# A hand-pipelined transformer block becomes a list of single-engine steps

## The chip, the cores and the metric

The kernel runs on one core of a Trainium2 chip. The metric is the device time of one execution in microseconds; the profiled execution also gives the span and every instruction's start and duration. The engines are PE (TensorE; PEld are its weight loads), DVE (VectorE), ACT (ScalarE), POOL (GpSimd) and SP (SyncE, which here only issues transfers). Each works through its own list of instructions.

## The reference

One block with a modulation from a condition vector: linear attention with softmax features, then a gated MLP that mixes along the sequence. S = 2048 rows, D = 448, 16 heads of 28, all in bf16.

```python
sa, ca, ga, sb, cb, gb = split(silu(c) @ w_mod, 6)
h = layernorm(x) * (1 + ca) + sa
q, k, v = split(h @ wqkv)
pq, pk = q @ w_phi, k @ w_phi                       # per head, 28 x 28
phi_q, phi_k = [softmax(pq), softmax(-pq)], [softmax(pk), softmax(-pk)]
kv, z = phi_k.T @ v, phi_k.sum(rows)
x = x + ga * ((phi_q @ kv) / (phi_q @ z + 1e-6)) @ wo
h = layernorm(x) * (1 + cb) + sb
zz = gelu(h @ w_in); z1, z2 = zz[:, :896], layernorm(zz[:, 896:])
x = x + gb * ((z1 * (w_sp @ z2 + b_sp)) @ w_out)
```

## The kernel before

`fast_path` does the work; `general_path` (not printed) runs only if a flag, read near the end, says that a bound is exceeded. Rows are 16 tiles of 128. Weights are folded on the chip: w_phi goes into wk and wq (`fold_T`, `fold_pf`), and the modulation goes into the weights. The scale 1+ca multiplies the rows of Wk, Wq and Wv, the shift sa becomes an extra row 64 of their last block through `fold_sa` and `bias_row`, and the transposed activations carry a one in column 448 (xpad, lines 578 to 580). For w_in, `win_bias` and `win_scale` do the same. `apply_ln` (L637) writes the normalised tile to xpad, and a DMA transpose on SP turns it into hT or h2T.

The order is written by hand. Setup runs to line 738. The k loop (L893) gives each tile k, v, their exps, sums (L762), reciprocal, phik (L766) and, two tiles later, the kv accumulation; loads, statistics of later tiles and weight folds are placed by tile number (`loads`, `late`). Half of q is done inside, the rest after it. `slot(j)` (L1042) is a software pipeline over tiles: num and its normalisation (L939 to 972), wo with the residual (L974), second layernorm, z2 (L1015) with bn_stats on DVE (L989) and the normalisation on ACT (L1012), z1 (L1030). Last come 28 g units of 16 matmuls (L1109) and the output products (L1118). The 32 w_sp transposes are issued on SP: five late in the k loop, eleven in the slots, sixteen before the g stage. Four one-bank and two two-bank PSUM buffers are handed out in rotation. The guard bounds the column norms of the folded weights (`norm_sq`, `norm_mm`).

Of the kernel before, what the change touches and what calls it, by code (L numbers as in the profile page):

```python
# [475 lines left out]
KB = [P, P, P, D - 3 * P + 1]  # L476
HP = 4
CB = HP * DH
BOUND = 1.9


def fast_path(tc, A_x, A_wqkv, A_w_phi, A_wo, B_w_in, B_w_sp, B_b_sp, B_w_out, c, w_mod, out, flag):

# [3 lines left out]
    NST = S // 512  # L489
# [17 lines left out]
    win_s = persist.tile([P, KC, 2 * FH], BF, name="f_win")
# [52 lines left out]


    nc.sync.dma_start(out=c_row[:], in_=c)
    nc.scalar.dma_start(out=x_sb[:, 0:2, :], in_=xv[:, 0:2, :])
    load_rows(nc.sync, wk_raw[:, :, 0:D], A_wqkv[:, D:2 * D])
    nc.scalar.dma_start(out=wm1[:, :, D:960], in_=wmod_v[:, :, D:960])
    with nc.allow_non_contiguous_dma(reason="small w_phi blocks"):
        nc.sync.dma_start(out=phi[:], in_=A_w_phi.rearrange("(g l) d f -> (l d) g f", l=4))
    nc.sync.dma_start(out=wm1[:, :, 0:D], in_=wmod_v[:, :, 0:D])
    load_rows(nc.sync, wv_raw, A_wqkv[:, 2 * D:3 * D])


    nc.vector.memset(warm[:], 0.0)
    nc.vector.memset(sbpad[:], 0.0)
    nc.scalar.activation(out=warm[:], in_=warm[:], func=ACT.Exp)
    make_identity(nc, ident[:])
    nc.gpsimd.memset(wk_raw[:, :, D:D + 16], 0.0)
    nc.gpsimd.memset(mhalf[:], -0.5)
    for r in range(4):
        nc.gpsimd.memset(xpad[r][:, D:512], 0.0)
        nc.gpsimd.memset(xpad[r][:, D:D + 1], 1.0)  # L580
    nc.gpsimd.memset(sapad[:], 0.0)
    with nc.allow_low_precision("0/1 masks are exact in bf16"):
        nc.vector.tensor_reduce(out=bmask[:], in_=ident[0:CB, 0:CB].rearrange("p (h f) -> p h f", h=HP), axis=AX.X, op=ALU.add)
        nc.vector.tensor_reduce(out=mask[:], in_=ident[:].rearrange("p (k h) -> p h k", h=HP), axis=AX.X, op=ALU.add)
    for s in range(2):
        nc.vector.tensor_copy(out=KVbd[:, s, :, :, 29], in_=mask[:].unsqueeze(1).to_broadcast([P, 4, HP]))

    def more_constants():
        for r in range(4, NX):
            nc.gpsimd.memset(xpad[r][:, D:512], 0.0)  # L590
            nc.gpsimd.memset(xpad[r][:, D:D + 1], 1.0)
        nc.gpsimd.memset(wq_raw[:, :, D:D + 16], 0.0)
        nc.gpsimd.memset(Wq[:, :, D:D + 16], 0.0)
        for r in range(3):
            nc.gpsimd.memset(pring[r][:, 2 * D:2 * D + 16], 0.0)
            nc.gpsimd.memset(vring[r][:, :, DH:DH + 1], 1.0)
        nc.gpsimd.memset(ones[:], 1.0)
        for r in range(NO):
            nc.gpsimd.memset(opad[r][:, D:512], 0.0)


# [12 lines left out]
    def keep_busy(n):
        wps = bank2("warm_ps")
        for _ in range(n):
            nc.tensor.matmul(wps[:, 0, :], lhsT=ident[:], rhs=sbpad[:].rearrange("p k m -> p (k m)"), start=True, stop=True)

    keep_busy(7)


    def stats_of(src, mv_t, tagp, pool):
        stats = pool.tile([P, nc.vector.BN_STATS_DIM], F32, tag=tagp + "st")
        nc.vector.bn_stats(out=stats[:], in_=src)
        nc.vector.bn_aggr(out=mv_t, in_=stats[:])

    def rstd_of(mv, n, tagp):
        rstd = sm.tile([P, 2], F32, tag=tagp + "rs")
        nc.gpsimd.tensor_scalar(out=rstd[:, 0:n], in0=mv[:, 0:n, 1], scalar1=LN_EPS, scalar2=None, op0=ALU.add)
        nc.gpsimd.tensor_tensor(out=rstd[:, 0:n], in0=rstd[:, 0:n], in1=mhalf[:, 0:n], op=ALU.pow)  # L630
        nmr = sm.tile([P, 2], F32, tag=tagp + "nm")
        for t in range(n):
            nc.gpsimd.tensor_scalar(out=nmr[:, t:t + 1], in0=mv[:, t, 0:1], scalar1=rstd[:, t:t + 1], scalar2=-1.0,
                                    op0=ALU.mult, op1=ALU.mult)
        return rstd, nmr

    def apply_ln(eng, i, rstd, nmr, t, dst):  # L637
        xp = xpad[i % NX]
        eng.tensor_scalar(out=xp[:, 0:D], in0=x_sb[:, i, :], scalar1=rstd[:, t:t + 1], scalar2=nmr[:, t:t + 1],
                          op0=ALU.mult, op1=ALU.add)  # L640
        nc.sync.dma_start_transpose(out=dst, in_=xp[:])

    l1mv, l1rs = {}, {}

    def l1_stats(i):
        if i % 2 == 0:
            l1mv[i // 2] = sm.tile([P, 2, nc.vector.BN_AGGR_DIM], F32, name="l1mv", tag="l1mv")
        stats_of(x_sb[:, i, :], l1mv[i // 2][:, i % 2, :], "l1", sm)

    def l1_rstd(q):  # L650
        l1rs[q] = rstd_of(l1mv.pop(q), 2, "l1")

    def l1_apply(i, eng):
        rstd, nmr = l1rs[i // 2]
        apply_ln(eng, i, rstd, nmr, i % 2, hT[:, :, i * P:(i + 1) * P])


    def fold_T(wraw, wT, act):
        tps = [bank_bf("tps") for _ in range(4)]
        for ms in ((0, 1, 2), (3,)):  # L660
            for g in range(4):
                for m in ms:
                    nc.tensor.transpose(tps[g][:, m * P:m * P + KD[m]], wraw[0:KD[m], m, g * CB:g * CB + P],
                                        ident[0:KD[m], 0:KD[m]])
        for g in range(4):
            if act or g % 2 == 0:
                nc.scalar.copy(out=wT[:, g, 0:D], in_=tps[g][0:CB, 0:D])
            else:
                nc.vector.tensor_copy(out=wT[:, g, 0:D], in_=tps[g][0:CB, 0:D])

    def fold_sa(wraw, wT):
        sa_ps = bank("sa_ps")
        for g in range(4):
            for kk in range(KC):
# [48 lines left out]
    for m in range(3):  # L723
        fold_pf(wTk, Wk, m, m % 2)
# [314 lines left out]
    def on(i):  # L1039
        return 0 <= i < NT  # L1040
# [164 lines left out]
```

## Time and profile before

| | |
|---|---|
| runs shown | 290.99, 290.8, 289.18 us (median 290.8) |
| span of the profiled execution | 288.6 us, 4323 instructions |
| transfers | 25.81 MB, of these 17.76 MB on SP's queue, 7.69 MB on ACT's |

The page gives no time for the profiled execution beside its span; the median run is 2.2 us above it. Section 1 of the page has busy time by engine, section 4 the chain of work that ended last, section 5 groups of instructions: busy us, mean ns of one, and after the bar the idle time before them with what ended it. Matmuls are pipelined, so a row's mean for one (379 ns for 512 columns) is longer than the distance between two (3.45 us for 16 in the chain).

### The profile page before, as it was taken

The numbers are of one execution on the slowest core, as the hardware profiler recorded it, in microseconds if no ns is written. First come the engines' busy times: TensorE is split into PE (matmuls) and PEld (weight loads), VectorE is DVE, ScalarE is ACT, GpSimd is POOL, SyncE is SP. The second block draws the span as 40 slices with busy tenths as digits, with TensorE's granted clock in tenths as the row PEclk, the third lists the DMA queues.
The fourth block names the chain that finished last, engine by engine and source line by source line (L and its number), as shares of the span: only waits on it lengthen the run. The fifth ranks groups of instructions, "written<-read, shape, count | busy, mean of one in ns | idle before, by whom it ended". The sixth has DMA issues, their size and how long they took to land.

```text
span 288.6 us, 4323 instructions
## 1 busy us (share of the span) xinstructions
PE 265.1 (92%) x1514; PEld 131.1 (45%) x1538; DVE 169.0 (59%) x353; ACT 111.2 (39%) x206; POOL 93.3 (32%) x197
## 2 busy tenths in 40 slices
PE   6688979995996989999999999999999999999991
PEld 3535544553442445444444444444444444444440
DVE  4587978798478799887754343334343343434333
ACT  2446648688684568676788800000000000000000
POOL 4544676620047667766554740000000000000000
PEclk9759999999798899999999999999999999999998
DMA  8929984384012765897635999000000000000102
GB/s 208 264 39 227 279 111 131 76 146 54 2 36 55 112 130 116 122 222 143 93 58 139 169 162 198 11 2 16 32 16 2 16 32 18 0 16 16 35 2 69
DMA packets 71088, 25.81 MB, mean 89 GB/s; under 512 B 61009, under 2 KB 70930, under 8 KB 71058
## 3 DMA queue, kind: packets, MB, share of 16 engines
q1 hardware_dynamic: 64098, 17.76, 34.6%
q10 hardware_dynamic: 6960, 7.69, 9.9%
q8 instruction: 14, 0.23, 0.4%
q14 instruction: 16, 0.13, 0.2%
HBM read 8.92 MB, written 1.84 MB: 37 GB/s over the span
## 4 chain that ended last, share of the span: by engine, by line
PE 75%; DMA 9%; DVE 8%; ACT 2%; issue 2%; POOL 1%; SPq 0%; DVEq 0%; ACTq 0%; POOLq 0%
PE g_ps L1113 33%; PE o_ps L1120 7%; PE z_ps L1034 7%; PE z_ps L1021 7%; PE k_ps L748 4%; PE x_ps L979 3%; DMA f_hT<-f_xpad 3%; PE q_ps L797 3%; PE v_ps L756 2%; DMA h2T<-f_xpad 2%; PE b_ps L705 2%; DMA f_phi<-in_A_w_phi_dram 2%; PE q_ps L784 2%; DVE sums L762 2%; PE kvacc L774 2%
## 5 line engine op out<-in xcount | busy, mean ns | idle before, releaser
L1113 PE MATMUL g_ps<-f_wsp,f_z2n 128*128 128x512 bf16 x437 | 97.9, 379 | 0.6
L1113 PEld LDWEIGHTS <-f_z2n 128*128 128x128 bf16 x448 | 43.8, 98 | 52.2
L1115 DVE TENSOR_TENSOR gb<-g_ps,f_bsp 128x512 f32<-128x512 f32 x28 | 19.4, 691 | 69.7 <-PE g_ps L1113 63.7
L1021 PE MATMUL z_ps<-f_win,h2T 128*128 128x448 bf16 (+1 forms) x128 | 28.4, 366 | 3.9 <-DVE t L966 3.4
L1034 PE MATMUL z_ps<-h2T,f_win 128*128 128x512 bf16 (+1 forms) x106 | 25.8, 380 | 0.5 <-issue 0.3
L968 POOL TENSOR_TENSOR f_opad<-t 128x448 bf16<-128x448 bf16 x16 | 16.5, 1031 | 25.3 <-DVE t L966 25.2
L989 DVE BATCH_NORM_STATS2 stats<-z2g 128x6 f32<-128x448 bf16 x32 | 18.3, 615 | 10.5 <-ACT z2g L1027 10.5
L1120 PE MATMUL o_ps<-f_wout,f_z1T 128*128 128x448 bf16 x112 | 23.3, 352 | 0.0
L1027 ACT ACTIVATE z2g<-z_ps 128x896 bf16<-128x896 f32 x16 | 14.7, 917 | 16.3 <-PE z_ps L1021 16.3
L1116 DVE TENSOR_TENSOR f_z1T<-gb,f_z1T 128x512 bf16<-128x512 f32 x28 | 19.7, 704 | 1.4
L762 DVE TENSOR_REDUCE sums<-f_E 128x32 f32<-128x896 bf16 x16 | 17.1, 1070 | 5.0 <-ACT f_E L751 4.9
L1021 PEld LDWEIGHTS <-h2T 128*128 128x128 bf16 (+1 forms) x128 | 12.3, 99 | 15.4 <-issue 3.2
L1012 ACT ACTIVATE f_z2n<-z2g,nm,rs 128x896 bf16<-128x896 bf16 x16 | 18.1, 1132 | 1.6 <-POOL nm L999 1.6
L966 DVE TENSOR_TENSOR t<-num,w 128x896 bf16<-128x896 f32 x16 | 17.5, 1091 | 1.5
L748 PE MATMUL k_ps<-f_Wk,f_hT 128*128 128x448 bf16 x64 | 16.1, 381 | 1.2 <-DMA f_hT<-f_xpad 0.7
L979 PE MATMUL x_ps<-f_wo,oT 128*128 128x448 bf16 x64 | 16.4, 354 | 0.6 <-DMA oT<-f_opad 0.4
L1120 PEld LDWEIGHTS <-f_z1T 128*128 128x128 bf16 x112 | 11.0, 98 | 10.9
L1034 PEld LDWEIGHTS <-f_win 128*128 128x128 bf16 x112 | 10.1, 97 | 12.8 <-issue 2.0
L756 PE MATMUL v_ps<-f_Wv,f_hT 128*128 128x448 bf16 x64 | 14.7, 354 | 0.9 <-DVE f_wTq L677 0.9
L1035 ACT ACTIVATE f_z1T<-z_ps 128x512 bf16<-128x512 f32 x28 | 15.1, 590 | 0.5 <-PE z_ps L1034 0.5
L766 DVE TENSOR_TENSOR f_phik<-f_E,r 128x896 bf16<-128x896 bf16 x16 | 12.6, 789 | 1.2
L996 POOL TENSOR_TENSOR rs<-rs,f_mhalf 128x2 f32<-128x2 f32 (+1 forms) x19 | 12.6, 664 | 1.6
(130 smaller groups left out, 331.6 us busy)
## 6 DMA issues: line engine op xcount, KB each, us to landing
out_dram<-ot SPq DMA_DIRECT2D x16, 112.0 KB, 1.7
f_x<-in_A_x_dram ACTq DMA_DIRECT2D x3, 448.0 KB, 4.8
f_win<-in_B_w_in_dram ACTq DMA_DIRECT2D x2, 672.0 KB, 6.0
f_wm<-in_w_mod_dram ACTq DMA_DIRECT2D x1, 840.0 KB, 6.8
f_wmg<-in_w_mod_dram ACTq DMA_DIRECT2D x2, 392.0 KB, 3.6
f_wout<-in_B_w_out_dram ACTq DMA_DIRECT2D x1, 784.0 KB, 5.4
f_wsp<-in_B_w_sp_dram SPq DMA_TRANSPOSE x32, 4.0
f_bsp<-in_B_b_sp_dram ACTq DMA_DIRECT2D x1, 512.0 KB, 3.8
```

Source lines behind the costliest of these rows:

```text
L748: nc.tensor.matmul(k_ps[:, 0:D], lhsT=hT[0:KB[kc], kc, i * P:(i + 1) * P], rhs=Wk[0:KB[kc], kc, :], start=(kc == 0), stop=(kc == KC - 1))
L756: nc.tensor.matmul(v_ps[:, 0:D], lhsT=hT[0:KB[kc], kc, i * P:(i + 1) * P], rhs=Wv[0:KB[kc], kc, :], start=(kc == 0), stop=(kc == KC - 1))
L762: nc.vector.tensor_reduce(out=sums[:], in_=E[:].rearrange("p s (c f h) -> p (s c) h f", c=4, h=HP), axis=AX.X, op=ALU.add)
L979: nc.tensor.matmul(x1[:, 0:D], lhsT=oT[0:KD[cc], cc, :], rhs=wo_s[0:KD[cc], cc, :], start=False, stop=(cc == KC - 1))
L989: nc.vector.bn_stats(out=stats[:, hf, :], in_=z2gs[i][:, hf, :])
L1012: nc.scalar.activation(out=z2n[:, i, :], in_=z2gs.pop(i)[:].rearrange("p a d -> p (a d)"), func=ACT.Identity, scale=rstd[:, 1:2], bias=nmr ...
L1021: nc.tensor.matmul(z_ps[:, hf, 0:D], lhsT=h2[0:KB[kc], kc, il * P:(il + 1) * P], rhs=win_s[0:KB[kc], kc, FH + hf * D:FH + (hf + 1) * D], s ...
L1034: nc.tensor.matmul(z_ps[:], lhsT=win_s[0:KB[kc], kc, fc * P:(fc + 1) * P], rhs=h2[0:KB[kc], kc, :], start=(kc == 0), stop=(kc == KC - 1))
L1113: nc.tensor.matmul(g[:], lhsT=z2n[:, s_, fc * P:(fc + 1) * P], rhs=wsp_tiles[tcn][:, s_, :], start=(s_ == 0), stop=(s_ == NT - 1))
L1115: nc.vector.tensor_tensor(out=gb[:], in0=g[:], in1=bsp[:, tsl], op=ALU.add)
L1116: nc.vector.tensor_tensor(out=z1T[:, fc, tsl], in0=gb[:], in1=z1T[:, fc, tsl], op=ALU.mult)
L1120: nc.tensor.matmul(o_ps, lhsT=z1T[:, fc, t * P:(t + 1) * P], rhs=wout_s[:, fc, :], start=(fc == 0), stop=(fc == FC - 1))
```

## The change

The body of `fast_path` is replaced. Each step becomes a function that runs on one engine, and a string, ORDER, lists 832 steps in the order in which they are issued; `/V`, `/S`, `/G`, `/Y` choose DVE, ACT, POOL or SP, `@A0` to `@A2` and `@B0`, `@B1` name the PSUM buffer (two banks or one).

- Layernorm's scale and shift are applied to the transposed tile in place (`fmod`: f1, f2), by DVE, ACT or POOL. The row of ones, the bias matmuls and the weight scalings go.
- Tiles 0 and 1 are transposed by PE (`X`) and scaled on the way out of PSUM (`XE`).
- Seven of the eight pieces of w_sp's first quarter (`W:0,u`) are loaded in the setup, ahead of the first DMA transpose of a tile (`T1:3`); w_sp's later quarters go into the space of Eq and hT.
- phik (`kP`) runs on POOL for nine tiles and on DVE for seven. The num normalisation (`nS`) runs for pairs of tiles, on POOL for two of eight pairs.
- The residual is added by PE for seven tiles (`wN`) and by DVE for nine (`wM`, `wR/V`). Sums for the second layernorm and for z2's come from accumulator outputs (`wR`, `wQ`, `zG`, `zQ`, the squares on ACT), moments from four small DVE steps for two tiles, the power on POOL; z2's normalisation (`zN`) is on DVE.
- The guard takes the largest of all softmax sums instead of the weights' norms, in the g stage.
- The last four output products end one after another.

```diff
-KB = [P, P, P, D - 3 * P + 1]
-BOUND = 1.9
+SUM_MAX = 4.0e12
+ORDER = """
+ld:c/Y ld:x0/S ld:wk/Y ld:wma1/S ld:x1/S du:4@A2 ld:phi/Y ld:x2/S m3 ld:wma2/Y ld:x3/S ct@B0 ld:wv/Y tbl m1 l1s:0 du:12@A2 m4 W:0,4 ce:1 ce:2 ce:3
+ce:4 W:0,2 l1r:0,1 FTk:0@B0 W:0,0 bd/G FTk:1@B1 l1a:0/V ETk:0/V W:0,5 X:0@A2 m2 ETk:1/S du:4@A1 l1s:1 cfA@B0 W:0,3 l1s:2 l1r:1,2 l1s:3 W:0,6 PFk:1@B1
+ec1 PFk:0@A1 l1r:2,4 l1a:1/V EPk:1/S PFk:2@A0 ec2 l1s:4 W:0,7 XE:0,3/S X:1@B0 PFk:3@B1 XE:0,0/S l1a:3/G EPk:2/V XE:0,1/S XE:0,2/V T1:3 EPk:3/S l1s:5
+vM:0@A2 EPk:0/S l1s:6 XE:1,3/S kM:0@B1 vC:0 l1s:7 XE:1,0/S ld:wq/Y kE:0 XE:1,1/V l1r:4,8 l1a:2/V kF:0 ld:x4/Y XE:1,2/V kM:1@B0 T1:2 ld:wo/S kS:0
...
+"""
+    def fmod(a, b, m, eng, sc, sh):
+        v = hT[:, m, a * P:b * P]
+        affine(eng, v, v, sc[:, m:m + 1], sh[:, m:m + 1])
+    def nS(j, eng):
+        cr, dn, w = crr[j % 2], dnr[j % 2], wr[j % 2]
+        eng.tensor_tensor(out=dn[:], in0=cr[:, :, 0, :], in1=cr[:, :, 1, :], op=ALU.add)
+        if eng is nc.gpsimd:
+            eng.tensor_tensor(out=dn[:], in0=dn[:], in1=mone[:].unsqueeze(2).to_broadcast([P, 2, H]), op=ALU.pow)
+        else:
+            eng.reciprocal(out=dn[:], in_=dn[:])
+        eng.tensor_tensor(out=w[:], in0=Sx[:, 2 * j:2 * j + 2], in1=dn[:].unsqueeze(2).to_broadcast([P, 2, 2, H]), op=ALU.mult)
+    def kP(i, eng):
+        eng.tensor_tensor(out=pr[i % NR][:, 0:2 * D].rearrange("p (a f h) -> p a f h", a=8, h=HP),
+                          in0=Er[i % NR][:].rearrange("p s (c f h) -> p (s c) f h", c=4, h=HP),
+                          in1=kr[i % 2][:].unsqueeze(2).to_broadcast([P, 8, DH, HP]), op=ALU.mult)
+    def zG(i):
+        nc.scalar.activation(out=stage_b()["z2g"][i % NZ][:], in_=ps["z" + str(i)][:, :, 0:D], func=ACT.Gelu_apprx_tanh, accum_out=zs1[:, i:i + 1])
+    def zQ(i):
+        nc.scalar.activation(out=junk[:], in_=later["z2g"][i % NZ][:].rearrange("p a d -> p (a d)"), func=ACT.Square, accum_out=zs2[:, i:i + 1])
+    for word in ORDER.split():
...
+            STEPS[nm](*[int(v) for v in arg.split(",") if v], **kw)
```

More of the change, by code (lines that the diff above doesn't have):

```diff
@@ L569, in fast_path @@
[L569 to L589, printed above, removed]
-            nc.gpsimd.memset(xpad[r][:, D:512], 0.0)
-            nc.gpsimd.memset(xpad[r][:, D:D + 1], 1.0)
-        nc.gpsimd.memset(wq_raw[:, :, D:D + 16], 0.0)
+    def load_phi(eng):
+        with nc.allow_non_contiguous_dma(reason="small w_phi blocks"):
+            eng.dma_start(out=phi[:], in_=A_w_phi.rearrange("(g l) d f -> (l d) g f", l=4))
@@ new lines, in ld, with consts @@
+    def ld(nm, eng):
+        LOADS[nm](eng)
+    def consts():
+        nc.vector.memset(one1[:], 1.0)
+        nc.vector.memset(warm[:], 0.0)
+        nc.vector.memset(zero[:], 0.0)
+        make_identity(nc, ident[:])
+        nc.gpsimd.memset(mhalf[:], -0.5)
+        for r in range(2):
+            nc.gpsimd.memset(xpad[r][:, D:512], 0.0)
+        nc.gpsimd.memset(hT[64:P, 3, 0:2 * P], 0.0)
+        with nc.allow_low_precision("0/1 masks are exact in bf16"):
+            nc.vector.tensor_reduce(out=bmask[:], in_=ident[0:CB, 0:CB].rearrange("p (h f) -> p h f", h=HP), axis=AX.X, op=ALU.add)
+            nc.vector.tensor_reduce(out=mask[:], in_=ident[:].rearrange("p (k h) -> p h k", h=HP), axis=AX.X, op=ALU.add)
@@ L619, in fast_path @@
[L619 to L648, printed above, removed]
@@ L735, in fast_path @@
-    l1_stats(4)
-    l1_stats(5)
-    l1_rstd(2)
-    l1_apply(4, nc.gpsimd)
-    Eq = eqp.tile([P, 4, 2, S], BF, name="f_Eq")
-    kvacc = bank2("kvacc")
-    qt = {}
-    def k_part(i):
-        k_ps = bank("k_ps")
-        for kc in range(KC):
-            nc.tensor.matmul(k_ps[:, 0:D], lhsT=hT[0:KB[kc], kc, i * P:(i + 1) * P], rhs=Wk[0:KB[kc], kc, :], start=(kc == 0), stop=(kc == KC - 1))
-        E = Ering[i % 3]
-        nc.scalar.activation(out=E[:, 0, :], in_=k_ps[:, 0:D], func=ACT.Exp)
-        nc.scalar.activation(out=E[:, 1, :], in_=k_ps[:, 0:D], func=ACT.Exp, scale=-1.0)
@@ L770, in kv_acc, with scb_copy, du @@
-    def kv_acc(i):
+        nc.gpsimd.memset(mone[:], -1.0)
+        nc.gpsimd.memset(ones[:], 1.0)
+        for s in range(2):
+            nc.gpsimd.tensor_copy(out=KVbd[:, s, :, :, 29], in_=mask[:].unsqueeze(1).to_broadcast([P, 4, HP]))
+        nc.gpsimd.memset(wo_s[64:P, 3, :], 0.0)
+        nc.gpsimd.memset(win_s[64:P, 3, :], 0.0)
+    def scb_copy():
+        nc.gpsimd.tensor_copy(out=scb[:], in_=scol[:].unsqueeze(2).to_broadcast([DC, KC, P]))
+    ps = {}
+    def du(n, slot):
+        wps = bank(slot, "warm_ps")
+        for _ in range(n):
+            nc.tensor.matmul(wps[:, 0, 0:256], lhsT=zero[:, 0:P], rhs=zero[:, 0:256], start=True, stop=True)
@@ new lines, in tbl, with ct, ctv, ce @@
+    def tbl():
+        nc.scalar.activation(out=warm[:], in_=warm[:], func=ACT.Exp)
+    def ct(slot):
+        t = ps["ct"] = bank_bf(slot, "ct_ps")
+        for kk in range(KC):
+            nc.tensor.transpose(t[0:DC, 2 * kk:2 * kk + 1], c_row[0:1, kk * DC:(kk + 1) * DC], one1[:])
+    def ctv():
+        return ps["ct"][0:DC, 0:8].rearrange("p (k t) -> p k t", t=2)[:, :, 0]
+    def ce(n):
+        if n == 1:
+            nc.scalar.activation(out=e[:], in_=ctv(), func=ACT.Exp, scale=-1.0)
+        elif n == 2:
+            nc.vector.tensor_scalar(out=e[:], in0=e[:], scalar1=1.0, scalar2=None, op0=ALU.add)
+        elif n == 3:
+            nc.vector.reciprocal(out=e[:], in_=e[:])
+        else:
+            nc.vector.tensor_tensor(out=scol[:], in0=e[:], in1=ctv(), op=ALU.mult)
@@ new lines, in kM, with kE, vM @@
+    def kM(i, slot):
+        t = ps["k" + str(i)] = bank(slot, "k_ps")
+        for m in range(KC):
+            nc.tensor.matmul(t[:, 0, 0:D], lhsT=hT[:, m, i * P:(i + 1) * P], rhs=Wk[:, m, :], start=(m == 0), stop=(m == KC - 1))
+    def kE(i, s):
+        nc.scalar.activation(out=Er[i % NR][:, s, :], in_=ps["k" + str(i)][:, 0, 0:D], func=ACT.Exp, scale=1.0 - 2.0 * s)
+    def vM(i, slot):
+        t = ps["v" + str(i)] = bank(slot, "v_ps")
+        for m in range(KC):
+            nc.tensor.matmul(t[:, 0, 0:D], lhsT=hT[:, m, i * P:(i + 1) * P], rhs=wv[:, m, :], start=(m == 0), stop=(m == KC - 1))
@@ L933, in fast_path, with qE @@
-    q_one(10)
-    q_one(11)
-    nums, sxs, oTs, h2Ts, x1s, z2ps, z2gs, mvs, rss = {}, {}, {}, {}, {}, {}, {}, {}, {}
-    def num_mm(i):
-        n_ps = bank2("num")
+            for m in range(KC):
+                nc.tensor.matmul(t[:, u, :], lhsT=Wq[:, m, cc * CB:cc * CB + P], rhs=hT[:, m, st * 512:(st + 1) * 512],
+                                 start=(m == 0), stop=(m == KC - 1))
+    def qE(n, s):
+        st, c2 = divmod(n, 2)
+        nc.scalar.activation(out=Eq[st // 2][0:CB, 2 * c2:2 * c2 + 2, s, (st % 2) * 512:(st % 2 + 1) * 512], in_=ps["q" + str(n)][0:CB, :, :],
+                             func=ACT.Exp, scale=1.0 - 2.0 * s)
@@ L1003, in l2_apply @@
-    def l2_apply(i, j):
-        st, il = divmod(i, 4)
-        if il == 0:
-            h2Ts[st] = sm2.tile([P, KC, 512], BF, name="h2T", tag="h2T", bufs=2)
-        rstd, nmr = rss[j]
-        apply_ln(nc.gpsimd, i, rstd, nmr, 0, h2Ts[st][:, :, il * P:(il + 1) * P])
-    def z2_norm(i, j):
-        rstd, nmr = rss[j]
-        nc.scalar.activation(out=z2n[:, i, :], in_=z2gs.pop(i)[:].rearrange("p a d -> p (a d)"), func=ACT.Identity,
-                             scale=rstd[:, 1:2], bias=nmr[:, 1:2])
@@ new lines, in wM, with wR @@
+    def wM(i, slot, with_x):
+        t = ps["x" + str(i)] = bank(slot, "x1_ps")
+        if with_x:
+            nc.tensor.matmul(t[:, 0, 0:D], lhsT=ident[:], rhs=x_sb[:, i, :], start=True, stop=False)
+        for cc in range(KC):
+            nc.tensor.matmul(t[:, 0, 0:D], lhsT=oTr[i % 4][:, cc, :], rhs=wo_s[:, cc, :], start=(cc == 0 and not with_x), stop=(cc == KC - 1))
+    def wR(i, eng):
+        t = ps["x" + str(i)][:, 0, 0:D]
+        if eng is nc.scalar:
+            nc.scalar.activation(out=x_sb[:, i, :], in_=t, func=ACT.Copy, accum_out=s1[:, i:i + 1])
+        else:
+            nc.vector.scalar_tensor_tensor(out=x_sb[:, i, :], in0=t, scalar=1.0, in1=x_sb[:, i, :], op0=ALU.mult, op1=ALU.add,
+                                           accum_out=s1[:, i:i + 1])
@@ new lines, in rpow, with l2a, T3, zM @@
+    def rpow(a, b, v):
+        nc.gpsimd.tensor_tensor(out=v[:, a:b], in0=v[:, a:b], in1=mhalf[:, 0:b - a], op=ALU.pow)
+    def l2a(i, eng):
+        eng.tensor_scalar(out=xpad[(NT + i) % NX][:, 0:D], in0=x_sb[:, i, :], scalar1=m2[:, i:i + 1], scalar2=v2[:, i:i + 1],
+                          op0=ALU.add, op1=ALU.mult)
+    def T3(i):
+        nc.sync.dma_start_transpose(out=hT[:, :, i * P:(i + 1) * P], in_=xpad[(NT + i) % NX][:])
+    def zM(i, slot):
+        t = ps["z" + str(i)] = bank(slot, "z2_ps")
+        for hf in range(2):
+            for m in range(KC):
+                nc.tensor.matmul(t[:, hf, 0:D], lhsT=hT[:, m, i * P:(i + 1) * P], rhs=win_s[:, m, FH + hf * D:FH + (hf + 1) * D],
+                                 start=(m == 0), stop=(m == KC - 1))
@@ new lines, in zN, with yM @@
+    def zN(i, eng):
+        z2n = stage_b()["z2n"]
+        eng.tensor_scalar(out=z2n[:, i, :], in0=later["z2g"][i % NZ][:].rearrange("p a d -> p (a d)"), scalar1=zm[:, i:i + 1], scalar2=zv[:, i:i + 1],
+                          op0=ALU.add, op1=ALU.mult)
+    def yM(st, fc, slot):
+        t = ps["y%d_%d" % (st, fc)] = bank(slot, "z1_ps")
+        for m in range(KC):
+            nc.tensor.matmul(t[:, 0, :], lhsT=win_s[:, m, fc * P:(fc + 1) * P], rhs=hT[:, m, st * 512:(st + 1) * 512], start=(m == 0), stop=(m == KC - 1))
@@ new lines, in yG, with W, gM @@
+    def yG(st, fc):
+        nc.scalar.activation(out=stage_b()["z1T"][:, fc, st * 512:(st + 1) * 512], in_=ps["y%d_%d" % (st, fc)][:, 0, :], func=ACT.Gelu_apprx_tanh)
+    def W(t, u):
+        q, hf = divmod(u, 2)
+        r0 = t * TCHF + q * P
+        nc.sync.dma_start_transpose(out=wspT[t][:, hf * 8:(hf + 1) * 8, q * P:(q + 1) * P], in_=B_w_sp[r0:r0 + P, hf * 1024:(hf + 1) * 1024])
+    def gM(t, fc, slot):
+        g = ps["G%d_%d" % (t, fc)] = bank(slot, "g_ps")
+        for s_ in range(NT):
+            nc.tensor.matmul(g[:, 0, :], lhsT=later["z2n"][:, s_, fc * P:(fc + 1) * P], rhs=wspT[t][:, s_, :], start=(s_ == 0), stop=(s_ == NT - 1))
@@ new lines, in gG, with oM @@
+    def gG(t, fc):
+        gb = later["gb"][fc % 2]
+        z = later["z1T"][:, fc, t * TCHF:(t + 1) * TCHF]
+        nc.vector.tensor_tensor(out=gb[:], in0=ps["G%d_%d" % (t, fc)][:, 0, :], in1=bsp[:, t * TCHF:(t + 1) * TCHF], op=ALU.add)
+        nc.vector.tensor_tensor(out=z, in0=gb[:], in1=z, op=ALU.mult)
+    def oM(t, f0, f1, slot):
+        if f0 == 0:
+            ps["o" + str(t)] = bank(slot, "o_ps")
+        for fc in range(f0, f1):
+            nc.tensor.matmul(ps["o" + str(t)][:, 0, 0:D], lhsT=later["z1T"][:, fc, t * P:(t + 1) * P], rhs=wout_s[:, fc, :], start=(fc == 0), stop=(fc == FC - 1))
@@ L1157, in fast_path @@
+    later["zp"].release()
+    psp.release()
+    eqp.release()
     persist.release()
-    return over
-TCHF = 512
+    return later["over"]
 def kernel(
```

758 lines of the change are left out of this document (300 added, 458 removed).

## The prediction

> **What bounds the kernel now.** I read the page first, then busy time by stage, the chain in order of time, the groups by form, the DMA rows and one stretch of the timeline. The page names the bound on average:
>
> ```profile
> PE 265.1 (92%) x1514; PEld 131.1 (45%) x1538; DVE 169.0 (59%) x353; ACT 111.2 (39%) x206; POOL 93.3 (32%) x197
> ```
>
> That average hides five stages. Their ends come from the timeline: first k matmul 15.6, first num matmul (KVbd is written) 77.6, first z2 matmul 92.4, first g matmul 164.7, last matmul 282.7 us.
>
> ```profile
> 0.00:15.60 15.60, 10.38 (x93) 6.69 (x94) 8.36 (x30) 5.28 (x10) 7.40 (x43) 0.83 0.96 219
> 15.60:77.60 62.00, 55.37 (x403) 30.34 (x409) 49.56 (x90) 41.23 (x74) 26.74 (x45) 0.93 0.60 124
> 77.60:92.40 14.80, 12.43 (x91) 6.10 (x90) 11.18 (x31) 10.96 (x30) 7.23 (x12) 1.00 0.17 39
> 92.40:164.70 72.30, 69.62 (x380) 33.36 (x387) 52.20 (x133) 52.09 (x92) 47.25 (x94) 0.98 0.70 129
> 164.70:282.70 118.00, 117.26 (x549) 54.57 (x558) 46.16 (x70) 1.61 (x2) 4.65 (x5) 1.00 0.20 36
> ```
>
> Columns: stretch, length, busy us (instructions) of PE, PEld, DVE, ACT, POOL, then granted clock, DMA share, GB/s. Only the fourth stretch (z) and the fifth (g) are PE's: in the g stage PE is busy for 117.3 of 118.0 us, while in the k stage it leaves 6.6 us idle, runs at a clock of 0.93, and DVE is at 80%. In the chain, setup and the k stage hang on transfers and on DVE:
>
> ```profile
> 7.42 8.15 DMA f_hT<-f_xpad
> ...
> 15.62 3.17 PE k_ps L748 x8
> ...
> 26.74 0.98 DVE sums L762
> ...
> 42.85 0.76 PE k_ps L748 x4
> ...
> 123.56 5.60 DMA h2T<-f_xpad
> ...
> 277.24 5.31 PE o_ps L1120 x28
> ```
>
> The first transpose waits 8.15 us behind earlier loads (median of that kind: 3.7); the first k matmuls take 3.17 us for 8, later ones 0.76 for 4, so the clock is at half there.
>
> ```profile
> L1012 ACT ACTIVATE f_z2n<-z2g,nm,rs 128x896 bf16<-128x896 bf16 x16 | 18.1, 1132 | 1.6 <-POOL nm L999 1.6
> L762 DVE TENSOR_REDUCE sums<-f_E 128x32 f32<-128x896 bf16 x16 | 17.1, 1070 | 5.0 <-ACT f_E L751 4.9
> L968 POOL TENSOR_TENSOR f_opad<-t 128x448 bf16<-128x448 bf16 x16 | 16.5, 1031 | 25.3 <-DVE t L966 25.2
> L996 POOL TENSOR_TENSOR rs<-rs,f_mhalf 128x2 f32<-128x2 f32 x13 | 9.2, 708 | 1.1
> L996 POOL TENSOR_TENSOR rs<-rs,f_mhalf 128x1 f32<-128x1 f32 x6 | 3.4, 568 | 0.5
> ```
>
> **The change, part by part.** I sum against this execution's span, 288.6 us; the runs shown have median 290.8, 2.2 above it, and I carry those 2.2 over.
>
> *PE work.* Gone: 20 bias matmuls (4 take 0.76: 3.8 us), 8 norm matmuls (1.5), 32 one-column ones (16 take 1.12: 2.2), 9 of 16 identity matmuls (0.19 each: 1.7). New: 8 small transposes (0.4). Warm-ups hold as many columns as before. That is 8.8 us less, but most lies in the k stage, which PE does not bound, so I credit it only through the stages below.
>
> *Setup and k stage.* Tiles 0 and 1 no longer wait for a DMA transpose; PE transposes them, so the first k comes some 3 us earlier. Behind them SP's queue now holds seven w_sp transposes ahead of T1:3 and T1:2, which tile 2 needs; the loads of wq and of x tiles 8 to 11 stand between those two. PE's order has the fold of wq, kv of tile 0 and k of tile 2 next, all behind these transfers, so PE will stand from about 20 to 28 us. Transfers before T1:14, the last one: 7.26 MB of loads at 269 GB/s (stretch 5 to 10 us) 27.0 us; 7 w_sp pieces at 1.51 us (ten were issued in 15.13 us from 155.5 on) 10.6; 14 tile transposes of 131 KB at 159 GB/s (that stretch's rate) 0.82 each, 11.5. Together 49.1; with the first issue and 2 to 3 us of landing, T1:14 is there at 52. Then three shift-and-scale steps on POOL (512 columns, from 0.71 for 448: 0.81 each), k and its exp (1.5), on DVE four times sums and reciprocal (1.07+0.35) and three phik (0.62), 7.5 us, the last kv matmuls and KVbd (2.2): 66.5. Bounds: DVE's own 16 tiles from 12 us on give 57; transfers at the landing time of a single piece instead (4.0 each) give 84. I take 66.5, nearer the issue spacing, since these pieces follow each other as those ten did.
>
> *POOL beside DVE.* Nine of 16 phik go to POOL, at twice L968's 1031 ns. One stretch shows a cost:
>
> ```profile
> 46.28 0.93 POOL L883 TENSOR_TENSOR f_wk_raw<-f_Wk 65x448 bf16<-65x448 bf16 x1
> ...
> 46.39 2.89 DVE L766 TENSOR_TENSOR f_phik<-f_E,r 128x896 bf16<-128x896 bf16 x1
> ...
> 47.20 0.70 POOL L639 TENSOR_SCALAR f_xpad<-f_x,rstd,nmr 128x448 bf16<-128x448 bf16 x1
> ...
> 47.87 0.93 POOL L883 TENSOR_TENSOR f_wq_raw<-f_Wq 128x448 bf16<-128x448 bf16 x1
> ```
>
> A DVE step of 0.62 took 2.89 while POOL ran three steps; the mean over 16 is 0.79, so 0.17 lost each with POOL busy 43%. With POOL at 80% and its steps about 2.5 times longer I scale to 0.8 us for each of 20 such DVE steps in this stage (16 us; bounds 3.4 at today's 0.17 and 45 at 2.27 each). Only those near the end of the stage are on the path: 4 us. KVbd at 70.5.
> The Trainium skill (SBUF — State Buffer, Who interferes with whom) says that a DVE step in a two-port mode, or with two SBUF inputs, and a GpSimd step exclude each other for the whole instruction. The 2.89 us agree; applied to every new DVE shift, scale and normalise it makes a rival below.
>
> *KVbd to the first z2.* One pair's path: num, Sx and cr (1.0), sums (0.64), two t (1.09 each), the add (1.03), transpose (2.5), two wo with residual (0.95 each), copies and squares (3.0), moments and pow (1.4), two applies (1.4), transpose (2.5), shift and scale (0.8): 17.7, and 1.3 for two w_sp pieces issued ahead on SP: 19.0, against 14.8. PE has 19 us of q, num and wo placed in it.
>
> *z stage.* PE: z2 24.3, z1 24.2, num 2.5, wo 6.4: 57.5. ACT: 16 gelu at 0.92, 16 squares at L1012's 1.13, 26 z1 gelu at 0.54 (spacing), 11 squares at 0.6, the rest 2.3, table 1.3: 57; the accumulator outputs have no row: between nothing and a small ACT step (0.185) on 45, I take half, 4. So ACT, 61, becomes the bound over PE. DVE loses the bn_stats of both norms (18.3 and 9.4 us) and gains 16 z2 normalises (half of the 1792-column scale's 1.02: 0.5 each, 8), 14 groups of four small moment steps (0.17 each, 9.5) and six residual adds (0.65, 4): 22 for 28, so it stays below ACT. Two nS on POOL raise 32 elements to a power: 0.71 if size did not matter, 4.9 by the 0.14 between L996's forms; I take the slope, and count what it delays: the t steps of tiles 10 to 13 wait for it on DVE, with shift-and-scale steps and x copies queued behind them, and PE's num of tiles 12 on for the banks that t frees. ACT has other work meanwhile, so 1.5 of the 8.4 is on the path; 2.5 for POOL against DVE. 65, against 72.3.
>
> *g stage and end.* The same 448 and 112 matmuls: 118.0. The guard is hidden: its reduces run while the next g unit (3.45) does. w_sp pieces now land in hT's and Eq's space; the last four blocks have 48 us to arrive. Tail 5.9, less 1.5 because three of the last four outputs no longer end behind the last matmul: 4.4.
>
> Sum: 70.5+19+65+118+4.4 = 276.9, 11.7 below 288.6; with the 2.2, 279.1 us.
>
> **Rivals.**
> *The list fits (faster).* Transfers overlap better, DVE bounds the k stage (57 + 3), 17 to z2, ACT without accumulator cost, 61: 60+17+61+118+4.4 = 260.4, timed 263. For it: the 0.60 DMA share of the k stage. Against: 1.13 in the stretches where transposes run.
> *Ports.* All 20 DVE steps of the k stage and as many of z pay 0.8 on the path: 8 more in k, 2 in z: timed 289, no change. That is also what the skill's rule gives if it holds throughout. For it: the 2.89 us. Against: ACT and transfers, not DVE, end these stages in my sum.
> *The queue (slower).* The seven w_sp pieces ahead of T1:3 cost their 4.0 us landing each, one after another: 28 instead of 10.6, tile 2 is at 45 and everything follows 17.4 later, 294.3, timed 297. It decides from 3.1 us a piece (1.51 + 11.2/7). For it: 8.15 us for the first transpose behind loads. Against: the ten pieces in 15.13 us.
>
> **How the numbers follow.** A measurement here tells about 1% from no change. Forecast 0.52, at 279, own range 271 to 287; the list fits 0.20; ports 0.12; the queue 0.16. So faster by over 1% 0.72, within 1% 0.12, slower 0.16. From 262 to 293 holds the forecast, the first two rivals: 0.84 less what lies beyond their ends.
>
> **What would show it.** Right: KVbd at 66 to 75 us, its start set by DMA f_hT; PE idle between tiles 1 and 2 until about 28; z2 normalise gone from ACT and ACT over 90% busy in z; the g stage still 118; a tail near 4.4. Wrong: tile 2's k before 22 (transfers not the gate); DVE phik or POOL phik far over 0.8 and 2.1 us; POOL's nS near 0.7; PE and not ACT full in z; gaps in the g stage behind w_sp.

## The result, and the profile after

The changed kernel takes 299.8 us (median of four; 296.5 to 301.3) against 290.0 for the kernel before on the same chip: ratio 1.028, 95% interval 1.021 to 1.036; the ratio leaves out the run of 301.3, which counts as slow beside the others. The change makes the kernel slower, where 279 us was forecast. The profiled execution, the quickest of the four, took 296.5; its span is 294.7 us, and the stages below explain that one. The page's first line of the kernel after, and its busy time by the same five stages (columns as before):

```profile
PE 262.4 (89%) x1488; PEld 134.0 (45%) x1488; DVE 163.3 (55%) x357; ACT 113.3 (38%) x242; POOL 102.5 (35%) x142
```
```profile
0.00:15.10 15.10, 11.79 (x97) 8.42 (x98) 8.65 (x26) 4.36 (x9) 11.09 (x46) 1.00 0.96 214
15.10:72.80 57.70, 48.79 (x329) 27.27 (x329) 42.40 (x80) 36.10 (x69) 35.82 (x37) 0.91 0.70 149
72.80:100.50 27.70, 21.91 (x182) 13.10 (x181) 21.10 (x51) 16.85 (x39) 15.35 (x18) 0.88 0.49 103
100.50:170.80 70.30, 61.73 (x327) 30.64 (x325) 41.36 (x126) 54.92 (x124) 40.21 (x42) 0.95 0.49 85
170.80:288.90 118.10, 118.10 (x562) 54.61 (x560) 49.11 (x76) 1.09 (x2) 0.00 (x0) 1.00 0.18 37
```

PE is busy for 2.7 us less in all (8.8 us less work was forecast; part of the time after is at half clock), and the span is 6.1 us longer: PE stands idle. In the z stage (fourth line) it was busy for 69.6 of 72.3 us and is now busy for 61.7 of 70.3. The third stretch, first num to first z2, has almost doubled, because the list puts more work into it and lets PE wait there. Against the forecast, by its own terms:

| term | before | forecast | after |
|---|---|---|---|
| first num matmul at | 77.6 | 70.5 | 72.8 |
| first num to first z2 | 14.8 | 19.0 | 27.7 |
| first z2 to first g | 72.3 | 65.0 | 70.3 |
| g stage to the last matmul | 118.0 | 118.0 | 118.1 |
| tail | 5.9 | 4.4 | 5.8 |
| span | 288.6 | 276.9 | 294.7 |

The groups by form and DVE's largest wait between 100 and 171 us name one loss at once (t is the DVE product that reads num out of its PSUM buffer, and so frees it; the columns of a wait are us in total, times, longest):

```profile
L905 POOL TENSOR_TENSOR f_dn<-f_dn,f_mone 128x32 f32<-128x32 f32 x2 | 11.0, 5477 | 0.2
```
```profile
DVE f_t L911 <- POOL f_w L908: 8.6, 2, 4.8
```

The power over 32 elements takes 5.48 us, twice; nearly four fifths of it (8.6 of 11.0) reappears as DVE waiting in front of its t products. PE's order of time shows the consequence:

```profile
118.66 0.58 PE L892 MATMUL num<-f_KVbd,f_Eq 112*128 112x120 bf16 x8 [2.46 <-DVE f_t L911]
...
130.38 3.14 PE L959 MATMUL z_ps<-f_win,f_hT 128*128 128x448 bf16 x8 [3.56 <-DVE f_t L911]
```

PE waits for the PSUM buffers that t frees, and after the longer wait eight z2 matmuls take 3.14 us where such a group takes 1.68: the clock has dropped to half (0.52 granted from 130.4 to 133.5). The Trainium skill (TensorE: Matmul & The Clock Gate, "What's actually happening") puts that drop behind some 3.4 us of idleness; the 3.56 us agree.

### The profile page after: what moved, and what is told of

The parts are those of the page before. It is cut to its first block, busy times and chain, and to the rows that moved or that the text cites. A ratio compares the mean times of both kernels' runs of the same rounds, so it can differ in the third digit from the quotient of the medians.

```text
span 294.7 us, 4158 instructions
## 1 busy us (share of the span) xinstructions
PE 262.4 (89%) x1488; PEld 134.0 (45%) x1488; DVE 163.3 (55%) x357; ACT 113.3 (38%) x242; POOL 102.5 (35%) x142
## 4 chain that ended last, share of the span: by engine, by line
PE 66%; POOL 10%; DMA 8%; DVE 7%; issue 3%; ACT 2%; SPq 2%; POOLq 0%; DVEq 0%
PE g_ps L1000 33%; PE z_ps L959 7%; PE o_ps L1012 7%; DMA f_hT<-f_xpad 6%; PE z_ps L987 6%; POOL f_dn L905 4%; PE q_ps L864 4%; PE x_ps L926 3%; DVE f_t L911 2%; DMA f_wk_raw<-in_A_wqkv_dram 2%; POOL f_hT L803 2%; POOL f_xpad L788 1%; POOL f_phik L837 1%; PE num L892 1%; POOL f_rs L784 1%
## 5 line engine op out<-in xcount | busy, mean ns | idle before, releaser
L1005 DVE TENSOR_TENSOR f_gb<-g_ps,f_bsp 128x512 f32<-128x512 f32 x28 | 19.3, 691 | 58.8 <-PE g_ps L1000 58.8
L1000 PE MATMUL g_ps<-f_Eq,f_z2n 128*128 128x512 bf16 x224 | 48.7, 379 | 0.0
L959 PE MATMUL z_ps<-f_win,f_hT 128*128 128x448 bf16 x128 | 27.5, 366 | 3.6 <-DVE f_t L911 3.6
L987 PE MATMUL z_ps<-f_hT,f_win 128*128 128x512 bf16 x112 | 27.2, 389 | 1.1 <-DVE f_dn L907 1.1
L1000 PE MATMUL g_ps<-f_hT,f_z2n 128*128 128x512 bf16 x112 | 24.7, 379 | 0.0
L1000 PE MATMUL g_ps<-f_wsp,f_z2n 128*128 128x512 bf16 x112 | 24.3, 379 | 0.0
L911 DVE TENSOR_TENSOR f_t<-num,f_w 128x896 bf16<-128x896 f32 x16 | 16.9, 1085 | 8.8 <-POOL f_w L908 8.6
L830 DVE TENSOR_REDUCE f_ksum<-f_E 128x32 f32<-128x896 bf16 x16 | 16.7, 1064 | 7.5 <-ACT f_E L819 7.5
L1006 DVE TENSOR_TENSOR f_z1T<-f_gb,f_z1T 128x512 bf16<-128x512 f32 x28 | 19.4, 692 | 1.2
L837 POOL TENSOR_TENSOR f_phik<-f_E,f_kr 128x896 bf16<-128x896 bf16 x9 | 16.0, 1772 | 5.7 <-DVE f_kr L834 3.1
L963 ACT ACTIVATE f_z2g<-z_ps 128x896 bf16<-128x896 f32 x16 | 14.6, 912 | 7.6 <-PE z_ps L959 7.6
```

Of the source, the lines that this page charges most:

```text
L830: nc.vector.tensor_reduce(out=ksum[:, i], in_=Er[i % NR][:].rearrange("p s (c f h) -> p (s c) h f", c=4, h=HP), axis=AX.X, op=ALU.add)
L837: eng.tensor_tensor(out=pr[i % NR][:, 0:2 * D].rearrange("p (a f h) -> p a f h", a=8, h=HP), in0=Er[i % NR][:].rearrange("p s (c f h) -> p ...
L911: nc.vector.tensor_tensor(out=tr[i % 2][:], in0=numv(i)[:, :, :, 0:DH], in1=wr[i // 2 % 2][:, i % 2].unsqueeze(3).to_broadcast([P, 2, H, D ...
L959: nc.tensor.matmul(t[:, hf, 0:D], lhsT=hT[:, m, i * P:(i + 1) * P], rhs=win_s[:, m, FH + hf * D:FH + (hf + 1) * D], start=(m == 0), stop=( ...
L987: nc.tensor.matmul(t[:, 0, :], lhsT=win_s[:, m, fc * P:(fc + 1) * P], rhs=hT[:, m, st * 512:(st + 1) * 512], start=(m == 0), stop=(m == KC ...
L1000: nc.tensor.matmul(g[:, 0, :], lhsT=later["z2n"][:, s_, fc * P:(fc + 1) * P], rhs=wspT[t][:, s_, :], start=(s_ == 0), stop=(s_ == NT - 1))
```

## The experiments

Ratios are against the kernel before on the same chip, with 95% intervals; the changed kernel stands at 1.028. Stage times are from each run's profile. Edits move or re-engine words of ORDER.

**The power on DVE.** Edit: `nS:5/G nS:6/G` become `nS:5/V nS:6/V`.

> Only edit: the two nS pairs on POOL (tiles 10 to 13) take DVE's reciprocal instead of POOL's power. Theory (the 5.5 us power stands on the path of the z stage twice, because DVE's t steps and PE's num wait for it): z stage 70.2 to 62-65 us, the run 5 to 8 us under the changed kernel's 299.8, so 292 to 295. Rival (ACT bounds the z stage, the power hides 6.9 of its 8.4 us): 1 to 2 us, 298 to 299.

Measured 0.994 (0.989 to 0.998). First z2 to first g in its trace:

```profile
101.60:164.10 62.50, 58.26 (x326) 28.93 (x323) 42.28 (x132) 54.77 (x124) 28.75 (x36) 1.00 0.56 95
```

70.3 became 62.5 us and PE is busy for 93% of it at a full clock. The two powers cost 7.8 us of this stage, of the 11.0 they run, and without them the whole loss against the kernel before is gone. ACT's 54.8 us are no bound.

**Place or operation?** On the changed kernel, with the two pairs still on POOL:

```diff
-        if eng is nc.gpsimd:
-            eng.tensor_tensor(out=dn[:], in0=dn[:], in1=mone[:].unsqueeze(2).to_broadcast([P, 2, H]), op=ALU.pow)
-        else:
-            eng.reciprocal(out=dn[:], in_=dn[:])
+        nc.vector.reciprocal(out=dn[:], in_=dn[:])
```

> On the changed kernel, only edit: in the two nS pairs on POOL the power is replaced by a reciprocal on DVE; the sum before it and the product behind it stay on POOL. Theory (the power's 5.5 us are the loss, not the place): z stage 62.5 to 65, the span 289 to 292. Rival (a pair that goes through POOL at all makes DVE and PE wait): z stage 67 to 70, the span 293 to 295.

Measured 1.001 (0.997 to 1.006), z stage 61.9 us, span 288.8. The operation is the loss; two trips through POOL are not.

**The w_sp pieces behind T1:14** (the last DMA transpose of a tile). Edit: the words `W:0,4 W:0,2 W:0,0 W:0,5 W:0,3 W:0,6 W:0,7` move from the setup to behind `T1:14`.

> Only edit: the seven w_sp pieces of the setup are issued after T1:14 instead of ahead of T1:3. Theory A (they hold up T1:3, T1:2 and wq by about 10 us): k of tile 2 at 23 or sooner instead of 29.5 and KVbd 4 to 6 us earlier, the run at 294 to 296. Rival B (POOL's statistics chain issues T1:3 late, DVE and POOL set the end of the k stage): tile 2 earlier by under 2 us, first num within 1.5 us of 72.8, the run at 298 to 300.

Measured 1.011 (1.000 to 1.022), span 295.6. T1:3 is issued at 14.6 instead of 20.3 us, k of tile 2 comes at 26.9 instead of 29.5, but T1:14 is issued only 2.4 us earlier, at 48.4, and PE gives that back: behind its last waits four v matmuls take 1.70 us instead of 0.92. The first num is at 73.0, as rival B has it, though tile 2 comes 2.6 us earlier and not under 2, and T1:3 did wait for the pieces. The median, 295.8 us, lies in theory A's range. The ratio lies lower than the changed kernel's and the intervals just overlap; a gain of a few us in time stays possible, the profiled spans show none.

**Gates early.** Edit: `scb gr:0 ge:0 wos:1 wos:3 wos:2 wos:0` move behind `kA:5` in the k stage, the seven `wts` (scalings of w_out) behind `gM:0,1`, the first g unit.

> Only edit: the attention gate (product gr:0, copy ge:0, the four wo scalings) is placed behind kA:5 in the k stage, the w_out scalings in the g stage, where POOL is idle. Theory (these steps stand ahead of the first num's normalisation on PE, ACT, DVE and POOL, 4 to 5 us of the 27.7 from num to z2): num to z2 23 to 24 us, the run at 295 to 296. Rival (PE's 19 us of q, num and wo and the transposes' round trip set that stretch): 27 us, 299 to 300.

Measured 1.030 (1.020 to 1.040): first num at 75.9, num to z2 27.1. The stretch is 0.6 us shorter and the first num 3.1 us later: nothing is won. The rival holds.

**Three together.**

> The three edits together. If each loss stands on the path by itself, they add: 5 to 8, 4 to 6 and 4 us under the changed kernel, 282 to 287, below the kernel before. If the stages share one bound (PE's list order) the sum is less than half of that: 292 to 297.

Measured 0.989 (0.978 to 1.000), 289.0 us: between the two ranges. It is the power's gain (0.994 alone) and little else.

**Transfers in order of need.** On top of the power on DVE: `ld:x4 ld:x5` go right behind `ld:wv`; win, the w_sp pieces, `ld:bsp ld:wmgb ld:wout` behind `T1:14`; the `wts` into the g stage.

> On top of the run with the power on DVE: x tiles 8 to 15 are loaded right behind wv, and win, b_sp, the second gate's weights, w_out and the seven w_sp pieces behind T1:14; the w_out scalings go to the g stage. Theory (transfers not needed in the k stage, about 4 MB, hold up tiles 8 to 15, and PE then has 18 us of dense work left after the last tile is there): first num at 67 to 70 instead of 73.6, the span 283 to 286. Rival (DVE and POOL, 40 and 36 us busy, pace the tiles): first num 72.5 to 74, the span 288 to 290.

Measured 0.977 (0.967 to 0.988). Its second and third stage:

```profile
15.80:69.28 53.48, 47.22 (x326) 26.39 (x324) 40.12 (x77) 35.41 (x66) 32.72 (x34) 0.91 0.69 153
69.28:96.85 27.57, 23.13 (x182) 13.73 (x181) 19.54 (x51) 16.87 (x39) 12.80 (x15) 0.81 0.50 103
```

The first num comes at 69.3 instead of 73.6, and the last tile transpose is issued by 44.8 us. So the order of the transfers does gate the k stage. In the changed kernel T1:14 is issued at 50.8 and lands at 54.0:

```profile
54.00:72.80 18.80, 17.60 (x143) 10.37 (x142) 14.41 (x26) 12.76 (x23) 12.84 (x11) 1.00 0.00 1
20.00:54.00 34.00, 27.11 (x174) 15.18 (x173) 23.94 (x44) 20.50 (x40) 20.56 (x22) 0.85 1.01 224
```

The two columns ahead of the last are granted clock and DMA share: until 54.0 the transfers are full and PE idles at a clock of 0.85, from then on nothing is transferred and PE works for 17.6 of 18.8 us. T1:14 itself is issued as soon as DVE has normalised tile 14 (49.67 to 50.80), a step that the list has behind the sums of tile 7; the transfers act through these earlier tiles. Taking the w_sp pieces out of the front alone was not enough; the whole reordering was. Which of its moves did it was not separated. Over all profiles the first num is at 67.0 to 71.2 in the six runs with these transfers, and at 72.4 to 74.2 in the six that have the changed kernel's loads and gates.

**All phik on DVE.** On top of the power on DVE: every `kP:i/G` becomes `kP:i/V`.

> On top of the power on DVE: all sixteen phik products on DVE, none on POOL. If POOL's phik cost DVE's steps 4 us on the path, as the prediction took it, the first num comes 2 to 4 us earlier, 70 to 72, and the span is 285 to 287. If they cost little (0.1 us a step), nine more products of 0.6 on DVE make no gain: 73.5 to 76, the span 289 to 292.

Measured 1.002 (0.998 to 1.006), first num at 74.2, span 289.3. Two groups of DVE steps, phik and the normalise of the tiles, first in the changed kernel, then here:

```profile
L837 DVE TENSOR_TENSOR f_phik<-f_E,f_kr 128x896 bf16<-128x896 bf16 x7 | 5.1, 733 | 0.2
L788 DVE TENSOR_SCALAR f_xpad<-f_x,f_nm,f_rs 128x448 bf16<-128x448 bf16 x7 | 5.1, 731 | 0.9 <-POOL f_nm L785 0.9
...
L833 DVE TENSOR_TENSOR f_phik<-f_E,f_kr 128x896 bf16<-128x896 bf16 x16 | 9.5, 611 | 0.3
L784 DVE TENSOR_SCALAR f_xpad<-f_x,f_nm,f_rs 128x448 bf16<-128x448 bf16 x7 | 3.0, 425 | 0.9 <-POOL f_nm L781 0.9
```

POOL's phik cost a DVE phik 0.12 us and a normalise 0.31 us, some 3 us for the fourteen steps, where the prediction had 16 for twenty. One of them is on the path: tile 14's normalise takes 1.13 us in the changed kernel, ending 0.1 us behind a phik on POOL, and 0.39 here. But with nine more products on DVE it starts later, and T1:14 is issued at 51.6 instead of 50.8. The trade is even; the run does not part its two sides.

**q between the num products.** On top of the power on DVE: `qM:4` to `qM:7` (products for q) go in turn between the `nM` (num products), in buffer A2, num in A1 and A0.

> On top of the run with the power on DVE (289.2 us span): q of tiles 8 to 15 (qM:4 to qM:7, 7 us of PE) is listed between the first num products instead of behind them, num takes the two other PSUM buffers in turn. Theory (the 28 us from num to z2 are PE's list order: it waits 5.8 us for DVE's t, at a granted clock of 0.88, and does q afterwards): num to first z2 22 to 24, the span 285 to 286. Rival (DVE's 18 us for eight tiles and the transposes' round trip set the first z2, so the wait only moves behind q): 27 to 28, the span 288 to 290.

Measured 1.020 (1.012 to 1.029), num to z2 35.0 us. Both expectations miss: q took a buffer from num, PE waited 5.2 us in all, three times, for the exps that free it, and the wo products fell behind. With the moved transfers as well:

> Both of these edits on top of the power on DVE. If both theories hold: first num at 67 to 70, z2 22 to 24 later, the span 279 to 283. If both rivals hold: 288 to 290.

Measured 0.990 (0.986 to 0.994): first num at 67.0, num to z2 31.6. The first half holds, the second does not.

**q in one-bank halves.** On top of the moved transfers: `qM:4` and `qM:5` become four products of one bank each, in B0 and B1, between the nums; the buffers of later steps shift with it.

```diff
+    def qh(n, u, slot):
+        st, c2 = divmod(n, 2)
+        t = ps["q%d_%d" % (n, u)] = bank(slot, "q_ps")
+        cc = 2 * c2 + u
...
+nM:0@A1 ... qh:4,0@B0 nM:2@A2 ... qh:4,1@B1 nM:3@A1 ... qh:5,0@B0 nM:4@A0 ... qh:5,1@B1
```

> On top of the same run (span 283.5): q of st 2 (qM:4, qM:5) is made in four one-bank halves, in the buffers that wo uses, between the first num products, so that num keeps its three two-bank buffers. Theory (PE's 4.4 us of waits between num products can hold q if it takes no buffer from num): num to z2 25 to 26 and the span 280 to 282. Rival (the exps of the halves stand ahead of num's x copies on ACT and DVE starts its t later, as in the run with q between the products): num to z2 28 to 30, the span 284 to 287.

Measured 0.972 (0.967 to 0.977). The num stretch of its trace:

```profile
69.10:94.50 25.40, 20.27 (x182) 11.60 (x181) 19.88 (x51) 16.91 (x43) 12.94 (x15) 1.00 0.57 112
```

2.2 us less than the 27.57 above. PE does as many matmuls in 20.3 us instead of 23.1, at a granted clock of 1.00 instead of 0.81. Its waits between the first nums fell from 1.36, 1.04 and 2.02 us to 0.49, 0.18 and 1.12, but a longer one is new, in front of the wo of tile 5:

```profile
90.64 0.93 PE L936 MATMUL x_ps<-f_wo,f_oT 128*128 128x448 bf16 x4 [2.25 <-DMA f_oT<-f_opad]
```

PE's idle time in the stretch is 5.1 us where it was 4.4, so what is gained is the clock. It is the fastest version here and beats both kernels; its interval overlaps that of the run it builds on.

**A shorter way for tiles 0 and 1.**

> On top of the run with the power on DVE and the transfers moved (span 283.5, num to z2 27.6): the steps on the way of tiles 0 and 1 come first. The wo scalings and DVE change places (all four on POOL), the adds of tiles 0 to 3 are on DVE (0.38 for 1.03), wN:0 and wN:1 stand ahead of nM:5 and nM:6 on PE, the modulation's second product behind wN:4, T3:1 and T3:0 ahead of two w_sp pieces on SP. Theory (the 8.7 us over my 19 are neighbours in the lists: 2.1 us of scalings ahead of the first cr, 1 us of adds, 4 us of num products that wait ahead of wo): tile 0's hT is there 5 to 6 us earlier and num to first z2 is 23 to 25, the span 280 to 282. Rival (PE has 21 us of other work listed ahead of the first z2, so an earlier tile waits for PE): num to z2 26.5 to 28, the span 283 to 284.

Measured 0.984 (0.976 to 0.991). The wo of tile 0 begins 6.2 us behind the first num instead of 8.8, yet the first z2 comes 29.6 us behind it, no sooner than before. The rival is right in kind; its 26.5 to 28 is passed. The same wish on top of the halves:

> On top of the run with q in one-bank halves (span 281.9, num to z2 25.4): T3:1 and T3:0 ahead of two w_sp pieces on SP, the adds of tiles 0 and 1 and the apply of tile 0 on DVE. If the way of tiles 0 and 1 now ends at the first z2 (PE's waits being filled), num to z2 23.5 to 24.5 and the span 280 to 281; if PE's list still ends there, 25 to 26 and 281 to 283.

Measured 0.975 (0.968 to 0.982), num to z2 28.7: PE waits 4.87 us for the transposes that wo of tiles 5 to 7 need, which SP now issues later. (Its first num is at 71.2, where the run with the halves, the same code up to there, gave 69.1. So a difference of 2 us between stages of two profiles shows nothing by itself, the 2.2 us of the halves run included; there the clock and PE's busy time stand beside it.)

**z2 ahead of those wo.** Edit on two bases, the halves and the run with only the power on DVE: `zM:0` (the first z2) goes behind `nM:8`, `W:1,0 W:1,3` behind `T2:7`; on the second base `qE:6` also moves ahead of `nM:8`.

> On top of the run with q in one-bank halves (span 281.9; there the last shift and scale of tiles 0 and 1 ended at 90.7 and the first z2 began at 94.5, behind wo of tiles 5 to 7, which waited 3.1 us for their transposes): zM:0 is listed right behind nM:8, ahead of wM:5 to wM:7, and two w_sp pieces behind T2:7 on SP. Theory (PE's order, not tile 0's way, sets the first z2): num to z2 21 to 22.5, the span 279 to 281. Rival (the work it passes is needed for the next tiles, so the z stage grows by as much): num to z2 as above, but num to g unchanged at 87.5 to 88 and the span 281 to 283.

> The same two moves on the run with only the power on DVE (span 289.2, num to z2 28.0, num to g 90.5; tiles 0 and 1 ready at 97.4, z2 at 101.6). Theory: num to z2 24 to 25 and num to g 87 to 89, the span 286 to 288. Rival: num to g 90 to 91, the span 288 to 290.

Measured 0.984 (0.972 to 0.997) and 1.005 (1.001 to 1.009). In the first, the third and fourth stage:

```profile
69.55:90.70 21.15, 17.11 (x160) 10.31 (x161) 18.31 (x45) 16.91 (x43) 12.03 (x14) 1.00 0.42 91
90.70:161.50 70.80, 62.97 (x337) 31.26 (x343) 44.84 (x137) 54.82 (x125) 30.32 (x39) 0.95 0.58 97
```

The first z2 comes 21.2 us after the first num, as the theory has it, and the z stage grows from 62.3 to 70.8; num to g is 91.9 instead of 87.7. On the other base it is 92.7 instead of 90.5. The border between the two stages moved; nothing was won, and in the first of the two PE now waits 5.3 us at once further on. The rivals expected no loss, so both go past them.

## Why the prediction was wrong

The profiled span lies 17.8 us over the forecast one: 8.7 between the first num and the first z2, 5.3 in the z stage, 2.3 up to the first num, 1.4 in the tail. The experiments show the step that failed in the z stage; the larger miss before it they show only in part.

**z stage, the step that experiments show to have failed.** It was "ACT has other work meanwhile, so 1.5 of the 8.4 is on the path". The size of the power was forecast well (4.9 by the slope, 5.48 measured), and so were those who wait for it: t on DVE, num on PE. But the cover was named on ACT, an engine that was not the bound. The engine that stands is PE, and with the power on DVE the stage loses 7.8 us: 7.8 on the path instead of 1.5. That PE and not ACT is full in z was one of the prediction's own signs of being wrong. The rest of the term erred the other way: ACT is busy for 54.9 us, not 61. z's squares take 948 ns where the normalise's 1132 was taken, 2.9 us less. An accumulator output is an instruction of its own near 0.19 us, 8.6 us for 45 where 4 was taken. The rows of ACT in this stage add up to 63.4 us, but they overlap each other; summing rows made ACT look like the bound:

```profile
L966 ACT ACTIVATE f_junk<-f_z2g 128x896 bf16<-128x896 bf16 x16 | 15.2, 948 | 0.1
L963 ACT ACTIVATION_READ_ACCUMULATOR f_z2g<-z_ps 128x1 f32 x16 | 3.1, 197 | 0.0
```

So without the power 62.5 us, PE-bound, under my 65.

**KVbd to the first z2, the larger miss.** The 19.0 were one pair's way (its pieces add up to 18.4 and not 17.7, so 19.7), with "PE has 19 us of q, num and wo placed in it" beside it, as though PE's work could run along. On PE's in-order list it can't: its first products in the changed kernel are

```profile
72.78 1.00 PE L892 MATMUL num<-f_KVbd,f_Eq 112*128 112x120 bf16 x16
75.14 0.58 PE L892 MATMUL num<-f_KVbd,f_Eq 112*128 112x120 bf16 x8 [1.36 <-ACT f_Eq L869]
77.73 0.59 PE L892 MATMUL num<-f_KVbd,f_Eq 112*128 112x120 bf16 x8 [2.01 <-DVE f_t L911]
78.72 0.98 PE L892 MATMUL num<-f_KVbd,f_Eq 112*128 112x120 bf16 x8 [0.40 <-DVE f_t L911]
81.72 0.98 PE L892 MATMUL num<-f_KVbd,f_Eq 112*128 112x120 bf16 x8 [2.02 <-DVE f_t L911]
```

From the third row on each group waits for the t that frees its buffer, and wo, the rest of q and z2 stand behind. From 78.7 to 84.0 the clock is at half (0.50 granted). PE's 21.9 us of work and 5.8 us of waits follow each other: 27.7. That the waits and the half clock have a share in the loss is likely from the halves run (PE's same work in 2.9 us less, the stretch 2.2 us shorter, no more than two profiles can differ by); it is not shown. Another part is where the list puts the border between the two stretches. Over both together, 84.0 were forecast; 98.0 were measured, 90.5 with the power on DVE, 87.7 with moved transfers and halves. What remains, 3.7 us, stays open; the other list orders tried against it moved it or made it worse.

**Setup and k stage.** 72.8 for 70.5, inside the band given, and T1:14 landed at 54.0 for 52. The last part was right by luck: from the landing to the first num 18.5 us were forecast and 18.8 measured, but not DVE's sums and products follow the last transpose, it is 17.6 us of PE work. (The steps named add up to 65.6 and not 66.5.) Of the 4 us for POOL beside DVE, 0.7 at tile 14's normalise (1.13 less 0.39) is what the traces show on the path. The start went nearly as told (PE stands from 20.3 to 25.5 us, k of tile 2 is at 29.5), and in the profile of the run with late w_sp an earlier start brings the first num no earlier.

**The rivals.** The queue gave 297, near the measured 299.8, but that is luck: its seven pieces were issued in 12.0 us, tile 2 was at 29.5 and not at 45. Ports is refuted at its place. The Trainium skill (SBUF — State Buffer, "Who interferes with whom") lets a DVE product with two SBUF inputs stand still while a POOL step reads SBUF, up to POOL's phik of 1.77 us. The trace agrees in kind: a DVE phik at 52.1 us, begun during POOL's, took 1.26 us, and where DVE began first, at 59.0 and 62.3, DVE took 0.58 and 0.60 and POOL's phik 1.87 and 1.90 instead of 1.69. The mean loss is 0.12 us for a DVE phik and 0.31 for a normalise, so the rival's price of 0.8 a step on the path is far too high.

**g stage, guard, tail.** 118.1, and the guard is hidden, as forecast. The tail came out at 5.8 us, for 5.9 before and 4.4 forecast: most of it is the way of the last output to memory, 5.0 us from the end of the last DVE step (289.7) to the end, 4.4 before.

## What to carry to other kernels

Where a long step is said to be covered, name the engine that bounds the stage and ask whether it has listed work in front of what waits; another engine's work is no cover. On in-order lists, waits for a ring of buffers add to the work behind them instead of running beside it, and a step brought forward gains only if nothing that it passes is needed just as soon. Transfers go in the order of need, measured by when the last one that a stage needs has landed.

## What was not expected of the hardware

The power on POOL grows with the elements of a partition: 0.58, 0.72, 1.04 and 5.48 us for 1, 2, 4 and 32, about 0.16 us each. And PE's clock was granted at 0.88 in the num stretch of the changed kernel, and at 0.81 in that of the run with the moved transfers, though no single wait there exceeds 2.02 us; in the halves run it was 1.00 beside a wait of 2.25 us. The Trainium skill (TensorE: Matmul & The Clock Gate, "What's actually happening") sets an idle window of some 3.4 us before the half clock; here waits that are each shorter, in close succession, stood before it, while a single one of 2.25 us was followed by full speed.
